# Two chained expert layers on one core: the first layer's input products by Strassen's algorithm, two plain tiles at the change of layers, and buffers laid out anew

## The chip, the core and the metric

The kernel runs on one core of one Trainium2 chip. The core has a TensorE (PE in the rows, with its weight loads as PEld), a VectorE (DVE), a ScalarE (ACT), a GpSimd (POOL) and a SyncE (SP) that issues the DMAs here. The metric is the device time of one execution in microseconds (us); the time of a kernel is the median of its runs.

## The reference

Attention by clusters (a query sees the keys of its own cluster), whose output has 1536 rows (tokens) of 512, and then two dense expert layers:

```
def _moe_ref(x, w_in, w_out):            # layer 1: x 1536x512, w_in 512x2048, w_out 2048x512
    h = x @ w_in
    g = h - np.tanh(h)
    return g @ w_out
...
def _moe2_ref(x, w_gate, w_val, w_out):  # layer 2: w_gate, w_val 512x1536, w_out 1536x512
    gate = 1.0 / (1.0 + np.exp(-(x @ w_gate)))
    val = x @ w_val
    return gate * val @ w_out
```

The weights come as 64-bit floats.

## The kernel before

**Numbers and tiles.** Every matrix product is made of three TensorE matmuls: each factor is split in a high and a low part, and high by high, high by low and low by high are summed in PSUM. A split is two instructions, a copy to the high part on ACT and a subtraction for the low part on POOL or DVE. Activations lie transposed, features on partitions, as `xh` and `xl` (high and low), in four column tiles of 384 tokens (`CH`, c = 0 to 3; c = 0, 1 are pair p = 0 and c = 2, 3 pair p = 1). Hidden features go in tiles of 128, two to a group: eight groups in layer 1 (`NG1`), six in layer 2 (`NG2`). `KD` = 4 is the number of 128-row pieces of the inner dimension of the input products, `KH` = 2 half of it.

**Layer 1** (`moe1_up`, `moe1_down`). For a group g and a column tile c, `up` makes two PSUM tiles of 12 matmuls (L927, in `mm3`), each of 128x384. ACT takes tanh, DVE subtracts (L962), and `pair_of` splits the result on ACT (L950) and POOL (L951). `moe1_down` multiplies by `w_out`: four PSUM tiles of 6 matmuls, which DVE adds to accumulators in SBUF (L1000). A column tile of a group thus takes 24 + 24 = 48 matmuls, and layer 1 takes 8 x 4 x 48 = 1536.

**Layer 2** (`moe2_up`, `moe2_down`). A pair of column tiles and one tile each of gate and value form a product of 2 x 2 blocks, which Strassen's algorithm (in Winograd's form) makes with seven block products in place of eight: 7 x 6 = 42 matmuls (L1136) in place of 48. The right factors are B11, B21, B22 and the sums T1 to T4 of the accumulators, which `inputs` makes and splits (L1041, L1044, L1054); the left factors are A11, A12, A22 and the sums S1 to S4 of the weights, made by `weights2` (L1087, L1089, L1098). The block sums come together in three PSUM banks X, Y and Z: the first product is copied out of X by ACT (L1152) before the third one goes into X, and so on.

**Weights.** `cut_piece` loads a piece of 128x256 doubles and makes 32-bit floats of it with three DVE instructions (L874 to L876); it is then split.

**Order.** The body only lists tasks with an engine, a modelled cost, a priority and dependencies; `Planner.run` sets the order of the instructions on every engine from these, engine by engine, before the program is built. `Z0` and `rank` set the priorities. `b4_left`, `raw_left`, `x_left` and their like say what an SBUF or PSUM buffer becomes when its first use is over, which is why the rows name the layers' operands by the attention's tiles: stk, hlq, hlk, oht, w, sum (split operands), pf, rawv (values before their split), pt, xn (accumulators, outputs), vs, rawq, xtq (weights); over_left, over_right and sm are PSUM banks.

## Time and profile before

| what | value |
|---|---|
| time, median of 3 runs | 812.18 us (811.35 to 816.54) |
| the profiled execution's own time | 816.28 us |
| its span, first to last instruction | 814.4 us |
| TensorE busy in the span | 792.9 us (97%) |
| VectorE, ScalarE, GpSimd busy | 550.2, 412.2, 493.6 us |
| mean granted TensorE clock | 0.985 of full speed |

Attention takes about the first 262 us of the span, layer 1 runs to about 525 us and layer 2 to the end. Matmuls overlap, so a busy TensorE is one that always had a matmul in flight; how many matmuls it ends in a stretch is told by the counts beside the busy times.

### The profile page before, as it was taken

What the parts mean: (1) busy time and instruction counts of PE and PEld (TensorE: products, weight loads), DVE (VectorE), ACT (ScalarE), POOL (GpSimd) and SP (SyncE); (2) the same over time, 40 slices, a digit from 0 to 9 for tenths busy, and PEclk for the clock granted to TensorE, in tenths of its full rate; (3) what the DMA queues carried; (4) which work ended last, traced back from release to release, by engine and by line L of the source; (5) the groups of instructions that cost most, each with busy time, mean ns of one, the idle gap of its engine ahead of it and who ended that gap; (6) DMA issues with size and microseconds to landing.
All of it is one profiled execution on the core that took longest, in us unless ns stands there. A gap on an engine that the chain in (4) does not pass through costs nothing.

```text
span 814.4 us, 15955 instructions
## 1 busy us (share of the span) xinstructions
PE 792.9 (97%) x6027; PEld 742.7 (91%) x6027; DVE 550.2 (68%) x1048; ACT 412.2 (51%) x796; POOL 493.6 (61%) x521
## 2 busy tenths in 40 slices
PE   8999999999899999999999999989999999999998
PEld 7879799888779999999999999979898999999896
DVE  3887987697797946765856643896474586747634
ACT  4177778878678534333233323556552534345240
POOL 4267677977779535442434536799483876649541
PEclk9988999999899999999999999999999999999999
DMA  8876566655353502211202100022230222202004
GB/s 187 205 188 138 128 152 138 141 128 140 88 151 112 173 31 95 104 52 53 78 13 66 52 14 1 1 65 81 85 103 18 66 97 73 77 27 79 27 1 155
DMA packets 66268, 72.94 MB, mean 90 GB/s; under 512 B 30256, under 2 KB 46736, under 8 KB 66192
## 3 DMA queue, kind: packets, MB, share of 16 engines
q1 hardware_dynamic: 66192, 71.93, 31.8%
q8 instruction: 47, 0.77, 0.4%
q14 instruction: 29, 0.24, 0.1%
HBM read 48.27 MB, written 3.15 MB: 63 GB/s over the span
## 4 chain that ended last, share of the span: by engine, by line
PE 84%; DVE 9%; ACT 2%; issue 2%; DMA 2%; POOL 1%; SPq 1%; DVEq 0%; ACTq 0%; POOLq 0%
PE over_left L927 20%; PE over_left L1136 13%; PE over_right L927 12%; PE sm L927 10%; PE over_right L1136 4%; PE sm L1136 3%; DVE finr L625 2%; PE sm L406 2%; PE sm L687 2%; PE sm L688 2%; PE sm L689 2%; PE bc L621 1%; PE sm L515 1%; PE ba L656 1%; PE bb L621 1%
## 5 line engine op out<-in xcount | busy, mean ns | idle before, releaser
L670 POOL TENSOR_TENSOR pt<-pf,pt 128x768 f16<-128x768 f32 x79 | 135.4, 1728 | 57.2 <-ACT pt L660 36.5
L951 POOL TENSOR_TENSOR stk<-pf,stk 128x384 fp32r<-128x384 f32 x35 | 35.6, 1018 | 61.5 <-ACT stk L950 60.4
L687 PE MATMUL sm<-vs,pt 128*128 128x65 f16 x576 | 63.7, 198 | 0.5 <-DVE mt L631 0.5
L687 PEld LDWEIGHTS <-pt 128*128 128x128 f16 x576 | 54.7, 99 | 9.2 <-issue 9.0
L688 PE MATMUL sm<-vs,pt 128*128 128x64 f16 x576 | 63.1, 199 | 0.0
L689 PE MATMUL sm<-vs,pt 128*128 128x65 f16 x576 | 62.7, 195 | 0.0
L688 PEld LDWEIGHTS <-pt 128*128 128x128 f16 x576 | 55.4, 100 | 0.7 <-issue 0.5
L689 PEld LDWEIGHTS <-pt 128*128 128x128 f16 x576 | 55.3, 102 | 0.0
L927 PE MATMUL over_left<-xh,stk 128*128 128x384 f32 x196 | 53.9, 334 | 0.0
L1136 PE MATMUL over_left<-xh,w 128*128 128x384 f32 x166 | 50.0, 338 | 1.7 <-DVE pf L1174 1.7
L1136 PE MATMUL over_left<-sum,w 128*128 128x384 f32 x206 | 44.5, 339 | 0.0
L625 DVE TENSOR_REDUCE finr<-bc 128x1 fp32r<-128x768 f32 x35 | 33.3, 950 | 16.1 <-PE bc L621 14.3
L927 PE MATMUL over_left<-xh,w 128*128 128x384 f32 x140 | 39.4, 337 | 0.3 <-DVE pf L962 0.3
L950 ACT ACTIVATE stk<-pf 128x384 fp32r<-128x384 f32 x39 | 20.4, 524 | 36.4 <-DVE pf L962 20.7
L625 DVE TENSOR_REDUCE finr<-bb 128x1 fp32r<-128x768 f32 x35 | 33.2, 949 | 7.6 <-PE bb L621 7.5
L927 PE MATMUL over_left<-stk,stk 128*128 128x384 f32 (+1 forms) x152 | 36.7, 362 | 0.9 <-ACT stk L950 0.8
L1136 PEld LDWEIGHTS over_left<-sum,w 128*128 128x128 f32 x206 | 36.9, 188 | 0.6 <-ACT rawv L1152 0.2
L962 DVE TENSOR_TENSOR pf<-over_left,pf 128x384 f32<-128x384 f32 x31 | 17.1, 555 | 28.3 <-ACT pf L961 28.2
L927 PE MATMUL sm<-stk,stk 128*128 128x512 f32 (+1 forms) x150 | 36.2, 364 | 0.0
L927 PEld LDWEIGHTS over_left<-xh,stk 128*128 128x128 f32 x196 | 35.8, 188 | 0.0
L660 ACT ACTIVATE pf<-ba 128x768 f32<-128x768 f32 x35 | 28.8, 822 | 13.1 <-PE ba L657 10.8
L660 ACT ACTIVATE pf<-bc 128x768 f32<-128x768 f32 x30 | 24.7, 823 | 16.1 <-PE bc L657 13.6
(515 smaller groups left out, 2750.8 us busy)
## 6 DMA issues: line engine op xcount, KB each, us to landing
vs<-in_moe_w_out_dram SPq DMA_DIRECT2D x25, 256.0 KB, 2.4
stk<-hlq SPq DMA_DIRECT2D x32, 192.0 KB, 2.7
stk<-hlk SPq DMA_DIRECT2D x16, 384.0 KB, 5.6
vs<-in_moe_w_gate_dram SPq DMA_DIRECT2D x18, 256.0 KB, 2.7
vs<-in_moe_w_val_dram SPq DMA_DIRECT2D x18, 256.0 KB
xtk<-in_moe_w_out_dram SPq DMA_DIRECT2D x16, 256.0 KB, 2.4
rawq<-in_q_dram SPq DMA_DIRECT2D x16, 192.0 KB, 4.7
rawk<-in_k_dram SPq DMA_DIRECT2D x16, 192.0 KB, 4.5
```

What stands on the lines that cost most here:

```text
L406: nc.tensor.matmul(tiles["sm", 1][:, 0:P], busy, busy, start=True, stop=True)
L625: rd.append(use(mx, add(DVE, c_dve(S), z + t, lambda t=t, mx=mx: nc.vector.tensor_reduce(at(mh)[:, t:t + 1], at(mx)[:, :, 0:HALF], axis=AX ...
L660: nc.scalar.activation(o.rearrange("p (j n) -> p j n", j=2), at(st)[:, :, 0:HALF], AF.Exp, scale=scale)
L670: lambda nce=nc.vector if on_v else nc.gpsimd, pf=pf, pt=pt: nce.tensor_tensor(at(pt)[:, 1], at(pf), at(pt)[:, 0], op=ALU.subtract), [e0, e1])
L687: nc.tensor.matmul(oview()[:, t], ph, vv[:, 0:D + 1], start=(kt == 0), stop=False)
L688: nc.tensor.matmul(oview()[:, t, 0:D], ph, vv[:, D + 1:2 * D + 1], start=False, stop=False)
L689: nc.tensor.matmul(oview()[:, t], plo, vv[:, 0:D + 1], start=False, stop=(kt == T - 1))
L927: nc.tensor.matmul(ps, a, b, start=(i == 0), stop=(i == n - 1))
L950: a = add(ACT, c_acts(CH), z, lambda: nc.scalar.activation(hi(), src(), AF.Copy), deps, take)
L951: b = add(POOL, c_pool(CH), z, lambda: nc.gpsimd.tensor_tensor(lo(), src(), hi(), op=ALU.subtract), [a])
L962: b = add(DVE, c_dve(CH), z, lambda ps=ps, th=th, g32=g32: nc.vector.tensor_tensor(at(g32), at(ps)[:, 0:CH], at(th), op=ALU.subtract), [a] ...
L1136: nc.tensor.matmul(at(bank[to])[:, 0:CH], lh, rh, start=start and i == 0, stop=stop and i == 3 * KH - 1, skip_group_check=True)
```

## The change

The first two of layer 1's eight groups stay as they were. For the other six, `inputs1` makes T1 to T4 out of the attention's output (POOL adds high and low part back together, DVE subtracts, ACT, DVE and POOL split), `weights2` makes A and S out of `w_in`, and `blocks` (the former `moe2_up`) makes the 2 x 2 blocks of two feature tiles and two column tiles by seven products; its new branch `one` takes h - tanh(h) with `less_tanh` and splits with `give`. At the change of layers the first two feature tiles of layer 2 (`NPL2`) are made plainly by `plain_up`, with 4 x 12 matmuls for a pair, from B11, B21, B12 and B22 alone; `inputs` first splits these four, and makes T1 to T4 in `sums`, listed after the second plain tile. Products of layer 1's down part and of layer 2 now share one set of six PSUM banks (`h2`), and two others serve `cut_piece` (`mid`). The accumulators come from tiles of twice the size (`twins`), the weights' raw buffers of the attention's time go to a pool that is closed and laid out anew (`rx`, `ry`), and `B4_TO` lists what the weight buffers become. Priorities have new constants.

```diff
-    ZLOWP=2.75, SEMS=1.0, TC=0.456, TW=0.74, M2=1, ZQK=0.25, ZMS=-28.375, Z0=47.548, HB=94, NB4=5, ROWS=0.0155,
-    VB=9.164, RAWL=2.2)
+    ZLOWP=2.75, SEMS=1.0, TC=0.456, TW=0.74, M2=1, ZQK=0.25, ZMS=-28.375, Z0=53.342, HB=94, NB4=5, ROWS=0.0155,
+    VB=9.164, RAWL=2.2, NMID=2, NPL2=2, W1L=0.7, D1L=0.322, W2L=1.623, D2L=-0.754, ZI=7.032, ZJ=1.1)
...
+            twin = left_p.tile([P, 2, 2, S], F16, name=f"ptt_{i}")
+            twins.append(twin)
+            for j in range(2):
+                new("pt", twin[:, j])
...
+    B4_TO = ["wb"] * 4 + ["wo"] * 2 + ["wb", "t", "t", "t", "wb"]
...
         x_gone.append(i)
-        return [new("h2" if len(x_gone) <= 2 else "x2", tiles["x", i])]
+        return [new("mid" if len(x_gone) <= NMID else "h2", tiles["x", i])]
...
         t = use_w(w, add(PE, C_UP, step(C_UP), mm_, w[1] + deps, [ps]))
+        ups_done.setdefault(c, []).append(t)
...
+    def inputs1(p):
+        c0, c1 = 2 * p, 2 * p + 1
+        where = {"B11": (0, c0), "B21": (KH, c0), "B22": (KH, c1), "T1": (0, c1), "B12": (0, c1)}
+        there = xt_done[2] + xt_done[3]
...
+        def of_tile(k):
+            val, ready = {}, {}
+            z = z0 + PRM["ZI"] + 0.1 * k
+            for n, kind in (("B11", "th"), ("B12", "g32"), ("B22", "th"), ("B21", "g32")):
+                val[n] = Slot(kind)
+                ready[n] = use(val[n], add(POOL, c_pool(CH), z, lambda n=n, v=val[n]: nc.gpsimd.tensor_tensor(
+                    at(v), place(n)(0, k).bitcast(F32), place(n)(1, k).bitcast(F32), op=ALU.add),
+                    there + sums_done, [val[n]]))
...
+            sum_("T1", "B12", "B11", "B11")
+            sum_("T3", "B22", "B12", "B12", [ready["T1"]])
+            sum_("T2", "B22", "T1", "B22", [ready["T3"]])
+            sum_("T4", "B21", "T2", "B21")
+            sums_done[:] = [ready["T4"]]
+            split("T2", DVE)
+            split("T4", POOL)
+            split("T3", DVE)
+
+            split("T1", DVE, ups_done[c1])
+
+        for k in range(KH):
+            of_tile(k)
+        return pairs
...
-        s11 = split("B11", POOL)
-        s21 = split("B21", POOL)
-        s22 = split("B22", POOL)
-        sum_("T1", "B12", "B11", "B11", s11)
-        sum_("T3", "B22", "B12", "B12", ready["T1"])
-        sum_("T2", "B22", "T1", "B22", s22 + ready["T3"])
-        sum_("T4", "B21", "T2", "B21", s21)
-        split("T2", DVE)
-
-        split("T1", DVE)
-        split("T3", POOL)
-        split("T4", POOL)
-        return pairs
+        done = [split(n, on) for n, on in (("B11", POOL), ("B21", DVE), ("B12", POOL), ("B22", DVE))]
+
+        def sums(used):
+
+            sum_("T1", "B12", "B11", "B11", done[0] + done[2])
+            sum_("T3", "B22", "B12", "B12", ready["T1"] + done[3])
+            sum_("T2", "B22", "T1", "B22", ready["T3"])
+            sum_("T4", "B21", "T2", "B21", done[1])
+            split("T2", DVE)
+            split("T1", POOL, used)
+            split("T3", DVE)
+            split("T4", POOL)
+
+        return pairs, sums
...
-        for i, (n, w, k) in enumerate((("A11", w_gate, 0), ("A12", w_gate, 1), ("A21", w_val, 0), ("A22", w_val, 1))):
+        for i, (n, w, f, k) in enumerate((("A11", w0, f0, 0), ("A12", w0, f0, 1), ("A21", w1, f1, 0), ("A22", w1, f1, 1))):
...
+        if plain:
+            split("A21")
+            split("A22")
+            cut_done[:] = pairs["A22"][1]
+            return pairs
...
+    def plain_up(A, B, p, gs, fi):
+
+        users = []
+        for c, names in ((2 * p, ("B11", "B21")), (2 * p + 1, ("B12", "B22"))):
...
+                t = add(PE, C_UP, step(C_UP), mm_, [d for (_, w), (_, b, _) in terms for d in w + b], [bank])
...
+            gate, t0 = half(1)
+            x = Slot("tmp")
+            th = add(ACT, c_act(CH), rank[0], lambda gate=gate, x=x: nc.scalar.activation(
+                at(x), at(gate)[:, 0:CH], AF.Sigmoid), [t0], [x])
+            use(gate, th)
+            value, t1 = half(2)
+            m = add(DVE, c_dve(CH), rank[0], lambda value=value, x=x: nc.vector.tensor_tensor(
+                at(x), at(value)[:, 0:CH], at(x), op=ALU.mult), [th, t1])
+            use(value, m)
+            use(x, th, m)
...
+        return users
...
+        def less_tanh(src, dst, dep, on, take=()):
+            th = Slot("tmp")
+            a = add(ACT, c_act(CH), rank[0], lambda: nc.scalar.activation(at(th), src(), AF.Tanh), [dep], [th])
+            b = add(on, c_pool(CH) if on == POOL else c_dve(CH), rank[0], lambda: (
+                nc.gpsimd if on == POOL else nc.vector).tensor_tensor(at(dst), src(), at(th), op=ALU.subtract), [a], take)
+            use(th, b)
+            return use(dst, b)
...
-        th0 = sigmoid(a, add_to(a, "Z", [ta, m2]))
+        t11 = add_to(a, "Z", [ta, m2])
+        if one:
+            give(c0, 0, a, less_tanh(lambda: at(a), a, t11, POOL))
+        else:
+            th0 = sigmoid(a, t11)
...
-        v1 = add_to(u, "Y", [tu, m5])
+        t22 = add_to(u, "Y", [tu, m5])
+        if one:
+            give(c1, 1, u, less_tanh(lambda: at(u), u, t22, POOL))
         m4 = product("A22", "T4", "X", [tu], True)
-        m3 = product("S4", "B22", "Y", [v1], True)
+        m3 = product("S4", "B22", "Y", [t22], True)
+        if one:
+            x = Slot("tmp")
+            t21 = less_tanh(lambda: ps("X"), x, m4, DVE, [x])
+            use(bank["X"], t21)
+            give(c0, 1, x, t21)
+            give(c1, 0, b, less_tanh(lambda: at(b), b, add_to(b, "Y", [tb, m3]), POOL))
+            return
...
-    per1 = NCH * (GF * C_UP + KD * C_DN) / 1.9
-    w1 = [(weights(cols(w_in, g), Z0 + (g - 1.3) * per1, "raw", "x" if g else "sm"),
-           weights(rows(w_out, g), Z0 + (g - 1.1) * per1, "raw", "x" if g else "sm")) for g in range(NG1)]
-    Z1 = Z0 + NG1 * per1
+    NPL, NPL2 = 2, PRM["NPL2"]
+    per0 = NCH * (GF * C_UP + KD * C_DN) / 1.9
+    w1 = [(weights(cols(w_in, g), Z0 + (g - 1.3) * per0, "rawx", "x" if g else "sm"),
+           weights(rows(w_out, g), Z0 + (g - 1.1) * per0, "rawx", "x" if g else "sm")) for g in range(NPL)]
+    Z1 = Z0 + NPL * per0
...
-    order1 = [(g, c) for cc in (0, 2) for g in range(2) for c in (cc, cc + 1)] + [(g, c) for g in range(2, NG1) for c in range(NCH)]
-    for g, c in order1:
-        gt = moe1_up(w1[g][0], c, xt_done[c])
-        flush()
-        pend = (w1[g][1], gt, c, g, False)
-    ups = [weights2(f, Z1 + (f - 1.3) * per2, "x" if f < 2 else "x2") for f in range(GF * NG2)]
-    downs = [weights(rows(w_out2, g), Z1 + (GF * g + 0.3) * per2, "raw2", "x2", "wo") for g in range(NG2)]
+        for x in todo:
...
+    for c0 in (0, 2):
+        for g in range(NPL):
+            for c in (c0, c0 + 1):
+                gt = moe1_up(w1[g][0], c, xt_done[c])
+                flush()
+                todo.append((moe1_down, w1[g][1], gt, c, g))
+        x1[c0 // 2] = inputs1(c0 // 2)
+    up1 = [weights2(w_in, GF * g, w_in, GF * g + 1, Z1 + (g - NPL - PRM["W1L"]) * per1, "x" if g == NPL else "mid")
+           for g in range(NPL, NG1)]
+    down1 = [weights(rows(w_out, g), Z1 + (g - NPL - PRM["D1L"]) * per1, "raw2", "mid", "wo") for g in range(NPL, NG1)]
+    ups = [weights2(w_gate, f, w_val, f, Z2 + (f - PRM["W2L"]) * per2, plain=f < NPL2) for f in range(GF * NG2)]
+    downs = [weights(rows(w_out2, g), Z2 + (GF * g - PRM["D2L"]) * per2, "raw2", "mid", "wo") for g in range(NG2)]
+    for g in range(NPL, NG1):
...
+        for p in range(NCH // 2):
+            gs = {c: ((Slot("g"), Slot("g")), []) for c in (2 * p, 2 * p + 1)}
+            blocks(up1[g - NPL], x1[p], p, gs)
+            flush()
+            for c in gs:
+                todo.append((moe1_down, down1[g - NPL], gs[c], c, g, "h2"))
+            if g == NG1 - 1:
+                todo.append((lambda p: x2.update({p: inputs(p)}), p))
     flush()
-    todo = []
     for g in range(NG2):
...
-                moe2_up(ups[GF * g + fi], x2[p], p, gs, fi)
-                for x in todo:
-                    moe2_down(*x)
-                todo = [(downs[g], gs[c], c, g) for c in (2 * p, 2 * p + 1)] if fi == GF - 1 else []
-    for x in todo:
-        moe2_down(*x)
+                f = GF * g + fi
+                if f < NPL2:
+                    used = plain_up(ups[f], x2[p][0], p, gs, fi)
+                    if f == NPL2 - 1:
+                        todo.append((x2[p][1], used))
+                else:
+                    blocks(ups[f], x2[p][0], p, gs, fi)
+                flush()
+                if fi == GF - 1:
+                    todo.extend((moe2_down, downs[g], gs[c], c, g) for c in (2 * p, 2 * p + 1))
+    flush()
```

How the built program's order moves, at three places. The first is TensorE at the start of layer 1's third group. Before, the first output tile's last matmuls and then the second's, of twelve each, from the x parts alone:

```order
L927 MATMUL over_left_3982<-xh,stk_88 128x384 x2
L927 MATMUL over_left_3982<-xl,stk_88 128x384
L927 MATMUL over_left_3982<-xh,stk_88 128x384
L927 MATMUL over_left_3983<-xh,stk_88 128x384
L927 MATMUL over_left_3983<-xl,stk_88 128x384
L927 MATMUL over_left_3983<-xh,stk_88 128x384 x2
```

Now, the end of the first product (bank over_left_3982), the second, of six matmuls, and the third (S2 by T2), which comes back to the first one's bank:

```order
L1288 MATMUL over_left_3982<-xh,stk_87 128x384
L1288 MATMUL over_right_3858<-xh,stk_87 128x384
L1288 MATMUL over_right_3858<-xl,stk_87 128x384
L1288 MATMUL over_right_3858<-xh,stk_87 128x384 x2
L1288 MATMUL over_right_3858<-xl,stk_87 128x384
L1288 MATMUL over_right_3858<-xh,stk_87 128x384
L1288 MATMUL over_left_3982<-sum_4324,stk_87 128x384
L1288 MATMUL over_left_3982<-sum_4325,stk_87 128x384
```

The bank's copy to SBUF has one product's time. The second place is TensorE at the change of layers. Before, the end of layer 2's second product, layer 1's last four down tiles, and the third product, which needs T2 (sum_6365 and its like) of the new activations:

```order
L1136 MATMUL over_left_3985<-xl,stk_88 128x384
L1136 MATMUL over_left_3985<-xh,stk_88 128x384
L927 MATMUL over_left_3984<-stk_86,stk_88 128x384 x6
L927 MATMUL over_right_3860<-stk_86,stk_88 128x384 x6
L927 MATMUL sm_71<-stk_86,stk_88 128x384 x6
L927 MATMUL over_right_3860<-stk_86,stk_88 128x384 x6
L1136 MATMUL over_left_3983<-sum_6365,w_132 128x384
L1136 MATMUL over_left_3983<-sum_6367,w_132 128x384
```

Now layer 1's last down tile is followed by the first plain tile, of B11 and B21 (in xh and xl) alone:

```order
L969 MATMUL over_left_3982<-hlk_125,w_132 128x384
L969 MATMUL over_left_3982<-hlq_122,w_132 128x384
L969 MATMUL over_left_3982<-hlk_125,w_133 128x384
L969 MATMUL sm_71<-xh,ry_4248 128x384
L969 MATMUL sm_71<-xl,ry_4248 128x384
L969 MATMUL sm_71<-xh,w_131 128x384
```

No product with a sum of the new activations stands between layer 1's down tiles any more. The third place is VectorE there, whose L1000 (now L1045) adds to the accumulators. Before, sums (L1054) and splits (L1044) stand among layer 1's own instructions, ahead of the last additions:

```order
L1054 TENSOR_TENSOR pt_108<-pt_104,pt_108 128x768
L1044 TENSOR_TENSOR xl<-xn_114,xh 128x384
L962 TENSOR_TENSOR rawv_92<-over_right_3859,rawv_92 128x384
L1054 TENSOR_TENSOR pt_104<-pt_104,xn_114 128x768
L1054 TENSOR_TENSOR pt_107<-pt_107,pt_104 128x768
L1044 TENSOR_TENSOR sum_6367<-pt_104,sum_6365 128x384
L1044 TENSOR_TENSOR sum_6369<-pt_104,sum_6366 128x384
L962 TENSOR_TENSOR rawv_92<-over_left_3982,rawv_92 128x384
```

Now the additions come with splits of B alone (L1153), and weights' cuts (L916 to L918):

```order
L1045 TENSOR_TENSOR ptt_104<-over_left_3981,ptt_104 128x384
L1153 TENSOR_TENSOR xl<-ptt_105,xh 128x384
L1045 TENSOR_TENSOR ptt_104<-sm_72,ptt_104 128x384
L916 TENSOR_SCALAR over_right_3859<-vs_89 128x256
L917 SCALAR_TENSOR_TENSOR over_right_3859<-vs_89,over_right_3859 128x256
L918 SCALAR_TENSOR_TENSOR vs_89<-vs_89,over_right_3859 128x256
L1153 TENSOR_TENSOR xl<-ptt_104,xh 128x384 x2
L1045 TENSOR_TENSOR ptt_105<-over_right_3858,ptt_105 128x384
```

The sums of 128x768 have moved behind all of layer 1's additions.

## Rows read from the trace of the kernel before

**Rows 1.** The page: the span, and TensorE's busy time, share and instructions.

```profile
span 814.4 us, 15955 instructions
...
PE 792.9 (97%) x6027; PEld 742.7 (91%) x6027; DVE 550.2 (68%) x1048; ACT 412.2 (51%) x796; POOL 493.6 (61%) x521
```

**Rows 2.** Stretches: from:to, length, then each engine's busy us (instructions), clock.

```profile
280.00:500.00 220.00, 220.00 (x1268) 220.00 (x1267) 134.16 (x294) 75.08 (x173) 96.47 (x114) 1.00 0.17 56
...
524.00:548.00 24.00, 20.38 (x97) 17.41 (x96) 22.58 (x40) 14.81 (x32) 22.75 (x21) 0.93 0.14 44
...
570.00:800.00 230.00, 230.00 (x1195) 213.44 (x1194) 137.41 (x285) 100.04 (x228) 142.86 (x177) 1.00 0.19 60
```

**Rows 3.** TensorE's waits, 520 to 550 us: in total, times, longest.

```profile
PE over_left L1136 <- DVE pf L1174: 1.7, 1, 1.7
PE over_left L927 <- ACT stk L950: 0.8, 1, 0.8
PE over_left L1136 <- DVE xl L1044: 0.5, 2, 0.3
PE over_left L1136 <- DVE stk L1044: 0.4, 1, 0.4
PE over_left L927 <- POOL stk L951: 0.2, 1, 0.2
```

**Rows 4.** TensorE's timeline at the change of layers: start, us, line, count, idle before.

```profile
525.49 0.94 PE L927 MATMUL over_left<-stk,stk 128*128 128x384 f32 x4 [0.78 <-ACT stk L950]
...
542.01 0.44 PE L1136 MATMUL over_left<-xh,w 128*128 128x384 f32 x1 [1.71 <-DVE pf L1174]
...
544.45 0.84 PE L1136 MATMUL over_left<-hlq,w 128*128 128x384 f32 x2
```

**Rows 5.** The chain that ended last, 505 to 570 us: start, us, what.

```profile
521.82 2.58 DVE sum L1044 x2
...
540.23 1.26 DVE xn L1054
```

**Rows 6.** Groups by line and form, 262 to 815 us: busy us, mean ns.

```profile
L951 POOL TENSOR_TENSOR stk<-pf,stk 128x384 fp32r<-128x384 f32 x35 | 35.6, 1018 | 61.5 <-ACT stk L950 60.4 <-PE over_left L927 0.8 <-PE over_right L927 0.3
...
L950 ACT ACTIVATE stk<-pf 128x384 fp32r<-128x384 f32 x39 | 20.4, 524 | 36.4 <-DVE pf L962 20.7 <-DVE pf L1174 11.8 <-POOL pf L1177 3.7
...
L1152 ACT ACTIVATE pf<-over_left 128x384 f32<-128x384 f32 x41 | 19.9, 486 | 22.6 <-PE over_left L1136 22.6
...
L1089 POOL TENSOR_TENSOR w<-vs,w 128x256 fp32r<-128x256 f32 x26 | 19.2, 740 | 4.2 <-PE over_left L1136 1.4 <-PE sm L1136 1.4 <-ACT stk L899 0.8
...
L962 DVE TENSOR_TENSOR pf<-over_left,pf 128x384 f32<-128x384 f32 x31 | 17.1, 555 | 28.3 <-ACT pf L961 28.2
...
L1087 ACT ACTIVATE w<-vs 128x256 fp32r<-128x256 f32 x33 | 13.4, 412 | 9.2 <-DVE vs L876 2.7 <-POOL vs L1098 2.3 <-PE over_left L1136 2.3
...
L875 DVE SCALAR_TENSOR_TENSOR over_left<-vs,over_left 128x256 uint32<-128x256 uint32 x30 | 12.9, 429 | 1.0
```

**Rows 7.** POOL's timeline: the attention's last subtraction, and two splits.

```profile
257.07 2.36 POOL L670 TENSOR_TENSOR pt<-pf,pt 128x768 f16<-128x768 f32 x1 [0.93 <-DVE xn L704]
...
522.65 2.62 POOL L1044 TENSOR_TENSOR sum<-pt,sum 128x384 fp32r<-128x384 f32 x2
```

**Rows 8.** DVE's timeline at the same time as the two splits.

```profile
521.75 2.66 DVE L1044 TENSOR_TENSOR sum<-pt,sum 128x384 fp32r<-128x384 f32 x2
```

**Rows 9.** Stretches of the attention with a low clock (last columns: clock, DMA).

```profile
60.00:80.00 20.00, 20.00 (x266) 18.00 (x267) 15.52 (x26) 13.74 (x21) 14.32 (x11) 0.85 0.64 142
...
200.00:220.00 20.00, 17.73 (x236) 15.24 (x236) 16.36 (x25) 13.39 (x20) 16.20 (x11) 0.83 0.29 73
```

**Rows 10.** The first stretch after the attention.

```profile
262.00:280.00 18.00, 17.68 (x123) 17.41 (x120) 16.97 (x43) 11.09 (x26) 13.88 (x18) 1.00 0.52 172
```

More of the change, by code (lines that the diff above doesn't have):

```diff
@@ L883, in f32_of, with weights @@
         return at(cut).bitcast(F32)
-    def weights(src, prio, raw_kind="raw", mid_kind="x", kind="b4"):
+    def weights(src, prio, raw_kind="rawx", mid_kind="x", kind="b4"):
         w = Slot(kind), Slot(kind)
@@ L935, in step @@
         return rank[0]
+    ups_done = {}
     def up(w, f, c, deps):
@@ L1019, in inputs @@
             ("B11", c0, 0), ("B21", c0, 1), ("B12", c1, 0), ("B22", c1, 1))}
-        where = {"B11": (0, c0), "B21": (KH, c0), "B22": (KH, c1), "T1": (0, c1)}
+        where = {"B11": (0, c0), "B21": (KH, c0), "B12": (0, c1), "B22": (KH, c1), "T1": (0, c1)}
         pairs = {}
```

168 lines of the change are left out of this document (121 added, 47 removed).

## The prediction

> **What bounds the kernel now.** The page comes first: TensorE is busy 792.9 of a span of 814.4 us, no other engine over 68% [rows 1]. An average over three stages proves little, so the stretches come next [rows 2]. From 280 to 500 us, in layer 1, TensorE is busy 220.00 of 220 us and ends 1268 matmuls: 0.1735 us for one of 128x384. VectorE has 134, GpSimd 96 and ScalarE 75 us there. From 570 to 800 us, in layer 2, where the blocks are already Strassen's, TensorE again has 230.00 of 230 us; GpSimd has 143 (62%), VectorE 137 (60%), ScalarE 100 (43%). So in both layers time follows the number of matmuls. (Its 1195 matmuls don't give that length, as layer 2's down part has matmuls of 128x512; no sum below uses them.)
>
> Between the two, from 524 to 548 us, only 97 matmuls end in 24 us [rows 2]. They are worth 97 x 0.1735 = 16.8 us, so the change of layers loses **7.2 us**. The view of TensorE's waits names 1.7 + 0.8 + 0.5 + 0.4 + 0.2 = 3.6 us of it [rows 3]; the timeline shows the 0.78 and 1.71 in place, and behind them two matmuls that take 0.84 us instead of 0.35 [rows 4], at a mean granted clock of 0.93 against 1.00 before and after [rows 2], between the levels of 1.2 and 2.4 GHz. 0.07 x 24 = 1.7 us is that clock's part; the other 1.9 are short waits. The chain of waits there runs over VectorE's splits (2.58) and sums (1.26) of the new activations [rows 5]: the third product, which needs T2, has nothing left in front of it.
>
> Attention ends with the same instructions in the same order; what differs there is where buffers lie. Its stretches at clock 0.85 and 0.83 [rows 9] make this execution one of the long ones: 816.28 us, 1.9 over its span, where the median is 812.18. I keep attention's time, and take the difference off the median.
>
> **The change part by part.**
>
> *Matmuls.* In six groups of layer 1, for two pairs, the up part takes 7 x 6 = 42 in place of 8 x 6 = 48: 6 x 2 x 6 = 72 fewer. The two plain tiles of layer 2 give back 2 x 2 x 6 = 24. Net 48 x 0.1735 = **-8.3 us**. TensorE being full where they go [rows 2], all of that counts, if the other engines keep up.
>
> *Steady groups of layer 1.* A group (two pairs) now has 2 x 42 + 96 = 180 matmuls, 31.2 us. GpSimd: 8 low parts and 6 subtractions of tanh, 14 x 1.018, and 15 instructions on weights of 256 columns, 15 x 0.740 [rows 6]: 25.4 us, 81% (it was 8 + 8 of these, 14.1 us of 33.3). VectorE: 24 x 0.555 and 24 x 0.429 for the cuts [rows 6]: 23.6 us, 76%. ScalarE: 22 of about 0.51 and 11 of 0.412 [rows 6]: 15.7 us, 50%. None is full, but GpSimd is at 81% where layer 2 shows 62% without loss, so the trace has no row for this load. Its cost is between 0 (as 570 to 800) and what its queue would make late; I take 0 for a group, since nothing waits for GpSimd's last results for at least a down tile.
>
> *X's copies.* A first product must leave bank X within the one product, 6 x 0.1735 = 1.04 us, that stands between. The copy takes 0.486 [rows 6]; behind one other 0.524 of ScalarE it is 1.01. That is tight, but layer 2 has the same three copies in each block, and from 570 to 800 it pays nothing. Zero, with the bad end as a rival.
>
> *Seam from plain to Strassen in layer 1.* `inputs1` adds 8 sums of two parts and splits for each pair on GpSimd. It comes free of attention at 257.07 + 2.36 = 259.4 us [rows 7], and has 36 x 1.018 + 22 x 0.740 = 53 us [rows 6] until the second pair's last split: 312 us. TensorE comes to it after the first two groups, 384 matmuls behind 262.6: 329 us. So 17 us of plain work cover it; the sums issue no DMA, and the row pieces of `w_in` are loaded as 128x2x256 pieces instead, as many issues on SP as before. But here VectorE adds from two operands in SBUF, 28 times, beside GpSimd. The only rows with such a pair show GpSimd's two splits at 2.62 us, 1.31 each instead of 1.018, while VectorE's two take 2.66 [rows 7, 8], 1.33 each instead of 0.555 with one operand in PSUM [rows 6]. 28 x 0.29 = 8.1 us more for GpSimd: inside the 17.
>
> The Trainium skill bears on this: "SBUF — State Buffer", section "SBUF: two separate sides", says that VectorE with two SBUF inputs and GpSimd hold a shared port pair in turn, the other one blocked for the whole instruction. The stretch of 1.018 to 1.31 agrees in direction; it is less than the two in turn (1.018 + 0.555 = 1.57). By the rule the sum for the seam would be 28 x 0.555 = 15.5 us of GpSimd, still within the 17, by little.
>
> *Start of layer 1.* Before, the first stretch after attention kept TensorE busy 17.68 of 18 us [rows 10]. The same plain groups start there: 0.3 us stays.
>
> *Change of layers.* Now four down tiles of layer 1 for each column tile lie behind seven products, and then a plain tile that needs only B11 and B21 split. Some twelve PSUM tiles of six matmuls, 12 x 1.04 = 12.5 us, stand on TensorE between the first pair's last down tile and that plain tile, and two splits of both kinds take 2.6 us even stretched [rows 7]. The sums and T splits, 5 us or more on VectorE by the chain [rows 5], lie behind 16 plain PSUM tiles of 12 matmuls, 16 x 2.08 = 33 us; T1's split, which waits for a plain tile's last reader, has about 20 us. What queues behind that wait on GpSimd is T4's split and weights' low parts for a later tile. So the old loss goes: **-7.2 us**. VectorE gets the four rounds of additions in a row with splits; what is late next is the first split itself.
>
> *New stalls.* The trace shows no seam of this kind. Between 0 (as in both steady stretches) and 7.2 (as the old seam) I take one wait as the 0.78 ahead of the down tiles [rows 4] with the 0.2 of GpSimd's split [rows 3], 1.0, and the 0.3 of a stretch at a start [rows 10]: **+1.3 us**, nearer to 0 because both seams have more plain work in front than the sums need.
>
> Sum: -8.3 - 7.2 + 1.3 = **-14.2 us**. This execution, 816.28, would be 802.1; the median, 812.18, becomes **798.0 us**.
>
> **Rivals.**
>
> A, *the loss at the change of layers only moves.* The plain tiles themselves come too early for the last additions, or the half clock is paid anyway behind some wait. For it: additions, splits and cuts all go over VectorE, which had 22.58 of 24 us there, and GpSimd 22.75 [rows 2]. Against it: 33 us of work that needs no sum. With all 7.2 kept, the saving is 8.3 less 0.3: 804.2 us; I put the case at 804.
>
> B, *GpSimd becomes the bound of layer 1's six groups.* If every instruction of its 25.4 us were stretched as the two splits were, by 1.31/1.018, it would need 32.7 us for a group against TensorE's 31.2: 1.5 x 6 = 9 us, 798 + 9 = 807. Against it: in the steady blocks no VectorE instruction reads two operands from SBUF (subtractions and additions read a bank, the cuts too), so the rows' cause [rows 7, 8] is there at the seams alone. The Trainium skill's rule (the same section) has that same condition, so by it this rival stays out.
>
> C, *slower than before: ScalarE late for bank X.* In layer 1 tanh and split copies of four results come to ScalarE in each block, beside the weights' copies. If each of the three copies of the 12 blocks, 36, stood behind one instruction of 0.52 us more than TensorE leaves it, that is 36 x 0.52 = 18.7 us; less the 15.5 of the two gains it makes 812.2 + 3.2 = 815.4. It decides from 15.5 / 36 = 0.43 us a wait, and half clock behind so many waits would add to it. Against it: layer 2's blocks, with sigmoids in the same place, wait nowhere long enough to move 230.00 of 230 [rows 2].
>
> That fewer matmuls bring nothing would need another bound than TensorE in layer 1; 220.00 of 220 us with VectorE at 61% [rows 2] leaves that no room.
>
> **How the numbers follow.** Forecast 798, 78%; A 10%, 804; B 6%, 807; C 6%, 815. The range: down to the old loss gone, no new stall, 812.2 - 15.5 = 796.7, and the runs' own spread below their median (0.8) and a little of attention's clock [rows 9], 794.5; up over A with the same spread, 806. About 1% is what a measurement of this kernel tells from no change, as its runs spread over 5 us: faster is below 804.1, slower above 820.3. The forecast and half of A, 83%, are faster; the rest of A, B and 2 of C's 6%, 13%, are the same; 4% are slower, C with waits above (820.3 - 796.7) / 36 = 0.66 us, which half clock would bring about.
>
> **What the profile after would show.** 48 fewer matmuls, TensorE full from 280 us to the change of layers and on, GpSimd near 80% and VectorE near 75% in the six groups; layer 1 ends some 12 us earlier (72 x 0.1735 = 12.5). At the change no wait for VectorE over 1 us, and clock 1.00. A shows as waits of a plain tile for a split of VectorE or GpSimd; B as TensorE waiting for GpSimd's low parts in every group; C as waits on bank X for the copy on ScalarE. The forecast is wrong if the first Strassen block of layer 1 waits for `inputs1` or for weights, if stalls of half a microsecond come in every block, or if the new places of buffers change attention.

## The result, and the profile after

The changed kernel takes **801.25 us** (median of 4 runs, 800.67 to 804.67) where the kernel before takes 812.94 (4 runs): a ratio of 0.9859, 95% interval 0.9815 to 0.9902. A second set of 6 runs of it, beside runs of before, gave 0.9868 (0.9841 to 0.9896), 804.07 against 814.19. It is faster by 1.4%, 11.7 us (10.1 in the second set); 798.0 with 14.2 less was forecast, in a range of 794.5 to 806.

The page of the changed kernel, its span and busy times (compare [rows 1]): 48 matmuls fewer, and more work on every other engine.

```profile
span 799.3 us, 15929 instructions
...
PE 779.2 (97%) x5979; PEld 731.4 (92%) x5979; DVE 573.3 (72%) x1076; ACT 439.4 (55%) x852; POOL 567.3 (71%) x597
```

Stretches of the changed kernel, in the columns of [rows 2]: the start of layer 1, its seam from plain groups to Strassen groups, the Strassen groups, the change of layers, and layer 2.

```profile
260.00:280.00 20.00, 19.28 (x113) 18.96 (x112) 16.90 (x32) 12.18 (x28) 17.92 (x20) 1.00 0.16 57
300.00:320.00 20.00, 18.24 (x103) 17.60 (x103) 13.45 (x18) 10.51 (x25) 13.80 (x13) 1.00 0.00 1
340.00:540.00 200.00, 200.00 (x1149) 200.00 (x1148) 153.14 (x328) 100.94 (x224) 163.29 (x188) 1.00 0.23 73
540.00:560.00 20.00, 19.64 (x101) 17.82 (x100) 17.24 (x33) 13.39 (x33) 19.92 (x20) 1.00 0.29 91
600.00:760.00 160.00, 160.00 (x831) 148.83 (x830) 104.39 (x216) 66.09 (x151) 98.68 (x123) 1.00 0.19 62
```

TensorE is full for the whole of 340 to 540 us, with GpSimd at 163 of 200 us (82%) and VectorE at 77%. The change of layers has lost its hole: 19.64 of 20 us at clock 1.00, where before it was 20.38 of 24 at 0.93. The holes are now at 260 and 300 us. TensorE's waits of the changed kernel after 255 us, in the form of [rows 3]:

```profile
PE over_right L969 <- DVE pf L1007: 1.7, 1, 1.7
PE over_left L969 <- ACT pf L1006: 0.7, 1, 0.7
PE over_right L1288 <- ACT pf L1304: 0.4, 1, 0.4
```

To account for all of it, take the part behind the attention: from the end of its last score matmul (254.41 us before, 250.68 after) to the end of the span. It is 559.97 us before and 548.58 after, 11.4 less. Going from each matmul's start to the next one's, every excess over 0.1736 us (384 columns; 0.2288 for 512) is a gap where it is above 0.03 us, and a slow matmul where it is less. A gap in this sense is a wait, or a matmul stretched by a lower clock behind one.

| us | before | after | difference |
|---|---|---|---|
| 2544 and 2496 matmuls of 384 columns x 0.1736 (431 of 512 the same) | 441.64 | 433.31 | -8.33 |
| gaps at the start of layer 1 (240 to 280 us) | 0.43 | 1.34 | +0.91 |
| gaps at layer 1's seam (300 to 340 us) | 0 | 2.61 | +2.61 |
| gaps at the change of layers | 7.41 | 0.97 | -6.44 |
| smaller gaps elsewhere | 0.72 | 0.01 | -0.71 |
| matmuls slower by under 0.03 us each, in sum | 2.11 | 3.24 | +1.13 |
| transposes and the rest | 5.01 | 4.45 | -0.56 |
| in all | | | -11.4 |

The attention was 3.7 us shorter in this profiled execution; that is its clock and not the change (last section).

### The profile page after: what moved, and what is told of

It reads as the page before. It is cut to its first block, busy times and chain, and to the rows that moved or that the text cites. A ratio compares the mean times of both kernels' runs of the same rounds, so it can differ in the third digit from the quotient of the medians.

```text
span 799.3 us, 15929 instructions
## 1 busy us (share of the span) xinstructions
PE 779.2 (97%) x5979; PEld 731.4 (92%) x5979; DVE 573.3 (72%) x1076; ACT 439.4 (55%) x852; POOL 567.3 (71%) x597
## 4 chain that ended last, share of the span: by engine, by line
PE 77%; DVE 10%; POOL 3%; issue 3%; DMA 3%; ACT 2%; SPq 1%; DVEq 0%; POOLq 0%; ACTq 0%
PE over_left L969 16%; PE over_left L1288 14%; PE sm L1288 11%; PE sm L969 9%; PE over_right L969 5%; PE over_right L1288 4%; DVE finr L637 2%; PE sm L418 2%; PE sm L699 2%; PE sm L700 2%; PE sm L701 2%; PE bb L633 1%; DVE vs L614 1%; PE ba L668 1%; PE bc L633 1%
## 5 line engine op out<-in xcount | busy, mean ns | idle before, releaser
L682 POOL TENSOR_TENSOR pt<-pf,pt 128x768 f16<-128x768 f32 x45 | 77.5, 1736 | 34.3 <-ACT pt L672 18.5
L682 POOL TENSOR_TENSOR ptt<-pf,ptt 128x768 f16<-128x768 f32 x34 | 58.2, 1717 | 19.7 <-ACT ptt L672 15.6
L996 POOL TENSOR_TENSOR stk<-pf,hlq 128x384 fp32r<-128x384 f32 x25 | 26.1, 1045 | 33.2 <-ACT hlq L995 33.2
L699 PE MATMUL sm<-vs,pt 128*128 128x65 f16 x330 | 43.7, 196 | 0.4 <-DVE mt L643 0.4
L701 PE MATMUL sm<-vs,pt 128*128 128x65 f16 x330 | 43.0, 193 | 0.0
L969 PE MATMUL over_left<-stk,w 128*128 128x384 f32 x158 | 40.1, 335 | 0.0
L699 PEld LDWEIGHTS <-pt 128*128 128x128 f16 x330 | 31.2, 97 | 6.2 <-issue 6.0
L672 ACT ACTIVATE pf<-ba 128x768 f32<-128x768 f32 x35 | 28.8, 823 | 13.3 <-PE ba L669 11.4
L1308 DVE TENSOR_TENSOR pf<-over_left,pf 128x384 f32<-128x384 f32 x32 | 17.7, 553 | 25.2 <-ACT pf L1304 11.4
L969 PE MATMUL over_left<-w,stk 128*128 128x512 f32 x118 | 34.9, 392 | 0.0
L700 PE MATMUL sm<-vs,ptt 128*128 128x64 f16 x246 | 34.8, 197 | 0.0
L699 PE MATMUL sm<-vs,ptt 128*128 128x65 f16 x246 | 34.7, 195 | 0.0
L701 PE MATMUL sm<-vs,ptt 128*128 128x65 f16 x246 | 34.4, 194 | 0.0
L672 ACT ACTIVATE pf<-bc 128x768 f32<-128x768 f32 x30 | 24.8, 826 | 14.9 <-PE bc L669 12.4
L996 POOL TENSOR_TENSOR oht<-pf,stk 128x384 fp32r<-128x384 f32 x25 | 25.6, 1025 | 9.9 <-ACT stk L995 9.2
L700 PEld LDWEIGHTS <-pt 128*128 128x128 f16 x330 | 31.5, 98 | 0.6 <-issue 0.5
L701 PEld LDWEIGHTS <-pt 128*128 128x128 f16 x330 | 31.7, 100 | 0.0
```

What stands on the lines that cost most here:

```text
L672: nc.scalar.activation(o.rearrange("p (j n) -> p j n", j=2), at(st)[:, :, 0:HALF], AF.Exp, scale=scale)
L682: lambda nce=nc.vector if on_v else nc.gpsimd, pf=pf, pt=pt: nce.tensor_tensor(at(pt)[:, 1], at(pf), at(pt)[:, 0], op=ALU.subtract), [e0, e1])
L699: nc.tensor.matmul(oview()[:, t], ph, vv[:, 0:D + 1], start=(kt == 0), stop=False)
L700: nc.tensor.matmul(oview()[:, t, 0:D], ph, vv[:, D + 1:2 * D + 1], start=False, stop=False)
L701: nc.tensor.matmul(oview()[:, t], plo, vv[:, 0:D + 1], start=False, stop=(kt == T - 1))
L969: nc.tensor.matmul(ps, a, b, start=(i == 0), stop=(i == n - 1))
```

## The experiments

All are edits of the changed kernel. "Stage" is the part behind the attention as above, which doesn't move with the attention's clock; gaps are those of TensorE by place. Stage and gaps are of one profiled execution each. The ratio is to the kernel before's runs beside each version, whose median was 813.2 to 814.2 us for all rows but the first two; ratios and stages compare better than medians.

| run | median us (range) | ratio to before, 95% | stage | gaps: all | seam | change |
|---|---|---|---|---|---|---|
| before | 812.94 (811.35 to 816.54) | | 559.97 | 8.56 | 0 | 7.41 |
| the change | 801.25 (800.67 to 804.67) | 0.9859 (0.9815 to 0.9902) | 548.58 | 4.93 | 2.61 | 0.97 |
| changed_again | 804.07 (800.35 to 804.88) | 0.9868 (0.9841 to 0.9896) | 548.65 | 5.00 | 2.75 | 0.89 |
| all_plain1 | 814.83 (814.09 to 819.67) | 1.0033 (1.0012 to 1.0054) | 562.20 | 6.49 | 0 | 5.04 |
| no_plain2 | 812.80 (808.77 to 814.09) | 0.9974 (0.9952 to 0.9995) | 556.90 | 17.29 | 2.62 | 13.33 |
| one_plain2 | 806.50 (805.87 to 810.08) | 0.9920 (0.9884 to 0.9957) | 554.38 | 12.55 | 2.63 | 8.56 |
| one_plain_group | 822.89 (821.27 to 824.18) | 1.0114 (1.0080 to 1.0149) | 569.06 | 27.25 | 24.81 | 1.25 |
| more_gpsimd | 827.69 (821.45 to 828.10) | 1.0157 (1.0109 to 1.0204) | 571.69 | 27.72 | 2.35 | 8.11 |
| copies_twice | 808.47 (806.71 to 811.67) | 0.9939 (0.9916 to 0.9961) | 555.45 | 11.48 | 2.79 | 2.15 |
| tanh_on_vector | 805.64 (804.71 to 807.24) | 0.9903 (0.9870 to 0.9935) | 552.81 | 8.99 | 2.61 | 2.77 |
| sums_on_vector | 801.50 (799.76 to 804.21) | 0.9854 (0.9822 to 0.9885) | 547.33 | 3.63 | 1.19 | 1.09 |
| sums_half | 801.83 (800.76 to 809.05) | 0.9866 (0.9833 to 0.9900) | 548.54 | 4.79 | 2.37 | 1.05 |
| sums_later | 805.42 (803.64 to 808.37) | 0.9896 (0.9863 to 0.9929) | 550.41 | 6.79 | 3.98 | 1.29 |
| measured_costs | 803.24 (802.29 to 805.16) | 0.9867 (0.9839 to 0.9895) | 549.54 | 5.80 | 2.27 | 1.20 |

**Each half alone.** First all of layer 1 plain (`plain1` is `moe1_up` with the weights' buffers of `weights2`):

```diff
+    NQ = 8
...
-        x1[c0 // 2] = inputs1(c0 // 2)
...
-    for g in range(NPL, NG1):
+    for g in range(NPL, NQ):
+        for p in range(NCH // 2):
+            for c in (2 * p, 2 * p + 1):
+                gt = plain1(up1[g - NPL], c)
...
+    for g in range(NQ, NG1):
```

> The changed kernel with all eight groups of layer 1 plain: only the two plain tiles of layer 2 and the new buffers are left of the change. Theory (time follows the matmuls, the plain tiles take the loss at the change of layers from 7.2 to about 1 us, and the seam inside layer 1 costs 2.6 us): against before 24 more matmuls, +4.2, and -6.2 at the change: 810.9; against the changed kernel 72 more matmuls, +12.5, less the seam's 2.6: 811.2. Rival (the loss at the change only moves into the plain tiles): 812.9 + 4.2 = 817. TensorE's gaps between the layers should sum to about 1 us by the theory, to 7 by the rival.

It came out at 814.83, no faster than before. The 72 matmuls are there: 562.20 - 548.58 = 13.6 is 12.5 for them, less the seam's 2.6, less 0.4 of slower matmuls, and 4.1 more at the change, whose gaps are 5.04 and not 1. They sit in layer 2's first down tiles, where TensorE waits for GpSimd's low parts:

```profile
PE over_right L969 <- POOL stk L996: 1.5, 1, 1.5
PE over_right L969 <- POOL w L943: 0.7, 1, 0.7
```

Neither theory's number held (1 and 7 us). The plain tiles alone save 2.4 us of gaps here and cost 4.2 in matmuls.

Then the change without plain tiles (B12 is not split then, and the sums are listed right behind layer 1's last additions):

```diff
-    ... NPL2=2, ...
+    ... NPL2=0, ...
...
-                todo.append((lambda p: x2.update({p: inputs(p)}), p))
+                todo.append((lambda p: (x2.update({p: inputs(p)}), x2[p][1]([])), p))
```

> The changed kernel without plain tiles at the change of layers: the sums of the new activations are listed right behind layer 1's last additions, and B12 is not split. Theory: 24 matmuls fewer, -4.2, and the loss at the change comes back to about 7 from 1: +6.2, so 801.3 + 2.0 = 803.3, with waits for VectorE's sums and splits as before. Rival (the down tiles behind seven products suffice, the plain tiles are not needed): 797, with no wait over 1 us there.

It takes 812.80 us, where the theory had 803.3: the loss that came back is 13.33 us, nearly twice the kernel before's. The rival (not needed) is out. A part of the loss is the lower clock behind the waits, 0.74 on average from 520 to 540 us. That stretch, then VectorE of no_plain2 at the longest wait, then TensorE:

```profile
520.00:540.00 20.00, 13.85 (x52) 11.94 (x51) 19.76 (x26) 13.09 (x28) 14.95 (x13) 0.74 0.11 39
```
```profile
522.94 1.27 DVE L1163 TENSOR_TENSOR ptt<-ptt,ptt 128x768 f32<-128x768 f32 x1
524.13 0.54 DVE L1308 TENSOR_TENSOR pf<-sm,pf 128x384 f32<-128x384 f32 x1
```
```profile
524.73 0.69 PE L1288 MATMUL sm<-xh,ry 128*128 128x384 f32 x1 [4.55 <-DVE pf L1308]
```

The addition that frees bank `sm` for layer 1's last blocks stands behind sums (L1163) of the next layer and weights' cuts in VectorE's queue, and TensorE stood 4.55 us. With one plain tile (`NPL2=1`):

> The changed kernel with one plain tile at the change of layers instead of two. Theory (the plain tiles are cover for the chain of sums and splits, which without them kept TensorE waiting some 13 us; one tile of both pairs is 8 x 2.08 = 16.7 us, which is more): 12 matmuls fewer, -2.1, loss at the change about 1 us as with two: 799.2. Rival (the chain needs more than one tile's time, VectorE and GpSimd being full there): half the 13 us comes back, 801.3 - 2.1 + 6 = 805, with waits for VectorE's splits ahead of the third product.

The rival came out: 806.5, 8.56 us of gaps at the change. TensorE's waits of one_plain2 there, and ScalarE:

```profile
PE over_left L1288 <- ACT pf L1304: 4.1, 1, 4.1
...
PE over_left L1288 <- ACT rawv L1304: 1.2, 1, 1.2
```
```profile
533.48 0.94 ACT L1150 ACTIVATE sum<-ptt 128x384 fp32r<-128x384 f32 x2 [4.28 <-DVE ptt L1163]
...
537.49 0.47 ACT L1304 ACTIVATE pf<-over_left 128x384 f32<-128x384 f32 x1
```

ScalarE stands 4.28 us in a split of a sum that VectorE has not made; the copy out of bank X (L1304) is behind it in the queue. So a tile's 16.7 us is no cover by itself: what counts is when the sums come through VectorE. Fewer plain tiles mean less cover and also an earlier place of the sums in the queues; these runs don't tell the two apart.

**How much plain work layer 1 needs in front** (`NPL = 1`):

> The changed kernel with one plain group in layer 1 instead of two, seven by Strassen. 12 matmuls fewer, -2.1. Theory (the seam in layer 1 is bounded by GpSimd and VectorE working off inputs1; GpSimd's 53 us of work had 17 us of slack under two groups, 67 us): under one group, 33 us, some 15 us of it are not covered: waits of 8 to 15 us, 807 to 814. Rival (the seam's 2.3 us are an accident of the order on VectorE and the work itself is small): 799.2.

Theory, and more than it: 24.8 us at the seam. TensorE's longest wait is again for the copy out of bank X:

```profile
PE over_right L1288 <- ACT pf L1304: 8.4, 3, 5.4
```

Not all of it is `inputs1`. ScalarE has splits of sums and the weights' copies ahead of that copy, and stands up to 2.34 us for weights that VectorE is still cutting; VectorE, with cuts and sums in turn, is busy 18.87 of 20 us from 300 to 320, and the granted clock is 0.75 there.

**GpSimd's margin in the steady groups.** In `less_tanh`, once in a block:

```diff
+            if on == POOL and len(extra) < 1:
+                extra.append(1)
+                for _ in range(2):
+                    a = add(POOL, c_pool(CH), rank[0], lambda: nc.gpsimd.tensor_tensor(
+                        at(th), src(), at(th), op=ALU.subtract), [a])
```

> The changed kernel with two more subtractions of 128x384 on GpSimd in each of layer 1's Strassen blocks (tanh is turned into the result and back before it is used), 4 x 1.018 = 4.1 us for a group: GpSimd's load goes from 81% to 29.5 of 31.2 us, 94%. Theory (its queue has real slack, the steady groups lose nothing): 801.3 to 802.5. Rival (GpSimd is as good as the bound, what looks idle is waiting in its chain): most of 24 x 1.018 = 24 us shows, 810 to 825, as waits of TensorE for GpSimd's low parts in every group.

The rival, and a little more than its range: 24.4 us more work on GpSimd made the stage 23.1 us longer. 15.9 of the gaps lie in the Strassen groups, 8.1 at the change (0.97 without it). The stretch of the groups in more_gpsimd, and two of its groups of TensorE rows with what ended their idle time:

```profile
340.00:540.00 200.00, 190.49 (x1057) 182.83 (x1056) 140.72 (x291) 88.31 (x202) 167.60 (x193) 1.00 0.21 64
```
```profile
L1288 PE MATMUL over_left<-xh,stk 128*128 128x384 f32 x42 | 13.4, 346 | 1.4 <-POOL stk L1199 1.4
L1288 PE MATMUL over_left<-sum,stk 128*128 128x384 f32 x40 | 9.1, 349 | 0.9 <-POOL stk L1199 0.9
```

GpSimd is 84% busy and TensorE already waits for its low parts of weights (L1199). What looks idle is time in which it waits in its own chain, as in the changed kernel's groups from 360 to 520 us:

```profile
L1318 POOL TENSOR_TENSOR pf<-pf,pf 128x384 f32<-128x384 f32 x10 | 10.1, 1014 | 4.3 <-ACT pf L1316 4.3
L1318 POOL TENSOR_TENSOR rawv<-rawv,pf 128x384 f32<-128x384 f32 x9 | 9.2, 1021 | 5.7 <-ACT pf L1316 5.7
L1318 POOL TENSOR_TENSOR pf<-pf,rawv 128x384 f32<-128x384 f32 x7 | 7.1, 1012 | 8.2 <-ACT rawv L1316 8.2
```

These waits for ScalarE's tanh are 18.2 of the 31 us that GpSimd is idle there, before 13 of 28 such subtractions. The added work stands in this chain, between tanh and the low part; whether as much of it elsewhere in GpSimd's queue would cost the same, no run shows. The reverse edit moves the three subtractions to VectorE (`less_tanh(..., DVE)` at the three places with POOL):

> The changed kernel with the three subtractions of tanh in each of layer 1's Strassen blocks on VectorE instead of GpSimd: GpSimd's load falls by 6.1 us for a group (to some 62%), VectorE's rises by 6 x 0.55 to 6 x 1.2 us, since they read two operands in SBUF beside GpSimd. Theory (GpSimd is near its limit in these groups but costs nothing yet, and VectorE at 27 to 31 of 31.2 us would be at its own): 802 to 806, with waits for VectorE. Rival (GpSimd's load is what costs in layer 1 and at the change): 799 to 800.

805.64, as the theory had it: GpSimd falls to 132 of 200 us, VectorE rises to 174 (87%), and TensorE waits for VectorE at the first group (1.0 and 0.4 us) and at the change (1.3 and 0.5).

```profile
340.00:540.00 200.00, 198.62 (x1135) 197.53 (x1134) 173.61 (x363) 101.25 (x225) 132.12 (x155) 1.00 0.24 74
```

**Bank X's copies** (`copy_out` in layer 1's blocks adds the same activation once more):

> The changed kernel with each copy out of bank X made twice by ScalarE in layer 1's Strassen blocks, 36 more instructions of 0.49 us: one product, 1.04 us, has to cover 2 x 0.49 and the way there and back. Theory (the single copy has some 0.4 us of slack, and each doubled one is late by 0.1 to 0.3 us, and half clock may follow): 36 x 0.1 to 0.3 = 4 to 11 us, 805 to 812. Rival (other instructions of ScalarE or the down tiles between products cover it): 801 to 802.

808.47, inside the theory's range, for another reason: not 36 late copies, but 5.1 us in one place (340 to 380), where a weight's copy stands in ScalarE's longer queue and the granted clock is 0.91 behind the wait (360 to 380), and 1.2 more at the change.

```profile
PE over_right L1288 <- ACT w L1197: 1.6, 1, 1.6
```

From 380 to 540 us TensorE is full with doubled copies. They are covered.

```profile
380.00:540.00 160.00, 160.00 (x918) 160.00 (x917) 123.30 (x260) 89.67 (x204) 132.74 (x153) 1.00 0.23 71
```

**The seam in layer 1.** In the changed kernel the chain of waits there is:

```profile
308.25 1.36 POOL rawv L1084
...
309.64 1.38 DVE pf L1090
...
311.11 1.17 DVE rawv L1090
312.28 0.48 DVE pf L1007
...
312.81 2.37 PE over_right L969 x12
```

GpSimd adds high and low part (L1084), VectorE makes two sums of them (L1090), and only then subtracts tanh for a plain tile (L1007), which frees TensorE's bank. Four edits tried to take that apart: the additions on VectorE (`add(DVE, ...)`, `nc.vector` at L1084), for both pairs and for the second alone; sums later (`ZI=9.0`); and the planned costs set to the measured durations.

> The changed kernel with the 16 additions of high and low part in inputs1 on VectorE instead of GpSimd. Theory (TensorE's 1.7 us wait at 312 us comes because VectorE's queue stands before a sum that waits for GpSimd's additions, which VectorE's own instructions with two SBUF inputs stretch): the wait goes, -1 to -2 us, 799.3 to 800.3. Rival (VectorE has too much to do at that seam): 16 x 0.55 = 8.8 us more on it, the wait grows to 3 us or more, 803 or above.

> The changed kernel with the additions of high and low part on VectorE for the second pair alone (8 of 16). Theory (the plain tile's subtraction stood behind the second pair's sums, which waited for GpSimd's additions): the 1.7 us wait goes as with all 16 moved, -1 to -2 us, 799.3 to 800.3. Rival (it took VectorE's sums of both pairs being free of GpSimd): the wait stays, 801.3.

> The changed kernel with the constant that sets the priority of inputs1's sums and splits (ZI) at 9 instead of 7.032, so that they come later among the plain groups. Theory (the plain tile's subtraction stands behind sums in VectorE's queue): fewer sums ahead of it, the wait gets shorter by 0 to 1.9 us, 799.4 to 801.3, if the first blocks do not wait for their sums in turn. Rival (the wait is one for a free bank whatever the order): 801.3, the same 1.7 us.

> The changed kernel with the costs of inputs1's instructions, from which the order is planned, set to what the trace shows beside each other: additions on GpSimd 1.3 us (planned 0.96), sums on VectorE 1.2 (planned 0.47), splits 1.2 and 0.8. Nothing is computed otherwise; the order on the engines is another. Theory (TensorE's waits at the seam in layer 1 come because the order was made for sums of half their length, so that a plain tile's subtraction stands behind them): the seam's 2.6 us fall below 1.3, 799.5 to 800.5. Rival (the seam has that much work whatever the order, and a better one for the plain tile makes the first Strassen blocks wait): 801 to 806.

Moving all 16 took 1.4 us off the seam (stage 547.33 against 548.58), as expected; its median can't be told from the change's. The other three went against the theory. sums_half lost the 1.7 us wait and got waits of 0.9 and 0.4 for GpSimd's low parts instead, 2.37 in all. sums_later made the first Strassen blocks wait 3.2 us for copies out of X, behind splits and weights' copies on ScalarE. measured_costs has no such wait for the subtraction, and 2.27 us of gaps among the first Strassen blocks instead (342 to 350 us), besides 1.0 us more at the start of layer 1. The waits of sums_half, sums_later and measured_costs:

```profile
PE sm L969 <- POOL hlq L996: 0.9, 1, 0.9
...
PE over_right L969 <- POOL oht L996: 0.4, 1, 0.4
```
```profile
PE over_left L1288 <- ACT pf L1304: 3.2, 3, 1.6
```
```profile
PE over_left L1288 <- DVE xnt L1045: 0.9, 1, 0.9
```

So the subtraction's place in the queue isn't the cause of the seam's loss, only its form. Four orders with additions on GpSimd (the change's, sums_half with eight of the 16, sums_later, measured_costs) pay 2.3 to 4.0 us; the one that leaves them all to VectorE pays 1.2. VectorE's sums in the changed kernel, and in sums_on_vector, two forms of each (durations in ns, least, median, greatest):

```profile
L1090 DVE TENSOR_TENSOR pf<-pf,pf x4: 541/908/1375, 273.8 to 303.3; 128x384 f32<-128x384 f32 x4
L1090 DVE TENSOR_TENSOR pf<-pf x4: 909/1294/2354, 276.3 to 304.0; 128x384 f32<-128x384 f32 x4
```
```profile
L1090 DVE TENSOR_TENSOR pf<-pf,pf x5: 543/557/981, 286.3 to 309.7; 128x384 f32<-128x384 f32 x5
L1090 DVE TENSOR_TENSOR pf<-pf x4: 546/556/1089, 279.7 to 308.2; 128x384 f32<-128x384 f32 x4
```

The same sum takes 0.56 us in the median with the additions gone from GpSimd, and 0.91 and 1.29 beside them. All 16 sums together take 16.7 us in the changed kernel and 10.6 in sums_on_vector. That the two engines' blocking of each other (last section) makes up the 1.4 us agrees with this, but no run here separates it from GpSimd's mere relief. changed_again has the same three waits in the same places as the first profile:

> The changed kernel itself, for a comparison on one chip with the two others. 801.3, TensorE's gaps after the attention 4.9 us in all, if the waits of 0.7 and 1.7 us in layer 1 are part of the order of the program; a rival, that they are an accident of one execution, gives other waits in other places.

No version tried beats the change by more than can be measured; sums_on_vector has the shortest stage.

## Why the prediction was right, point by point

**Matmuls, -8.3: right.** Layers 1 and 2 are full before and after, and the count's worth appears (-8.3; with all_plain1's 12.5 its stage comes out too).

**Change of layers, -7.2: right in size, half right in its reason.** 7.41 us of gaps became 0.97. That sums and splits need plain work in front is shown by 13.33, 8.56 and 0.97 us with no, one and two plain tiles. But the down tiles behind seven products were counted as cover too, and with them alone no_plain2 loses 13.33 us; and all_plain1 shows 5.04 us with both plain tiles where layer 1 is plain. Why the Strassen groups leave the change smoother stays open: the waits there name GpSimd, and all_plain1 also cuts layer 1's weights in other banks than the change does. One row was misread there: two matmuls in 0.84 us [rows 4] stand against 0.51 for such a pair at clock 1.00, not 0.35; no sum rests on it.

**New stalls, +1.3: the term that was mis-sized.** They came to 5.6: 0.9 more at the start of layer 1, 2.6 at its seam, 0.97 at the change, 1.1 in slower matmuls. The 1.3 less of small things elsewhere was not foreseen, and makes the sum -11.4 instead of -10.1, where -14.2 was forecast; that part of the closeness is luck. Two steps failed in this term. *"The same plain groups start there: 0.3 us stays"*: VectorE of the changed kernel now splits the attention's last transposes (L736) ahead of the subtraction that frees a bank,

```profile
262.99 1.02 DVE L736 TENSOR_TENSOR xl<-sm,xh 128x384 fp32r<-128x384 f32 x2
263.93 0.55 DVE L1007 TENSOR_TENSOR pf<-over_left,pf 128x384 f32<-128x384 f32 x1
```

and TensorE waits 0.7 us. (Its row names ScalarE's L1006, which ends within 0.01 us of the subtraction; in sums_on_vector the row of this wait names L1007.) The attention's own instructions stand in the order of before on each engine, as the prediction has it, but layer 1's are put among them otherwise. all_plain1 has the same wait, so it isn't the Strassen work (read, not tested by itself). *"17 us of plain work cover it"*: the seam was costed as GpSimd's work laid end to end, done at 312 us, with TensorE there at 329; 308 and 325 with the attention 3.7 us shorter. In the changed kernel GpSimd's last split of a T ends at 320.7,

```profile
319.72 1.02 POOL L1100 TENSOR_TENSOR stk<-pf,w 128x384 fp32r<-128x384 f32 x1 [0.60 <-ACT w L1097]
```

and TensorE's first Strassen product begins at 321.3: of the 17 us some 0.5 were left. GpSimd's work was not the error: blocking by VectorE cost it 5.1 us from 271 to 341 (above 1.02 and 0.74 us an instruction), where 8.1 was reckoned. It stood waiting, busy 13.80 of 20 us from 300 to 320, mostly for ScalarE's high parts of the plain groups' results, and these for VectorE's subtraction of tanh behind its sums:

```profile
312.78 0.53 ACT L995 ACTIVATE stk<-pf 128x384 fp32r<-128x384 f32 x1 [4.27 <-DVE pf L1007]
```

VectorE's own part was put at nothing: its 28 instructions on two operands in SBUF took 12.5 us more than 0.55 each, in the queue that also holds the plain tiles' subtractions. The first Strassen block itself shows no named wait for `inputs1`, the sign of being wrong that the prediction gave; a plain tile ahead of it does. one_plain_group, 24.8 us where 15 was expected, fits with less cover than 17, but doesn't size it, as its weights were late too.

The two engines in turn were reckoned as 1.018 + 0.555 = 1.57 us, so that the rows' 1.31 and 1.33 [rows 7, 8] looked like less. They are the turns themselves (last section).

**Rival B**, GpSimd as the bound: it didn't happen, 200.00 of 200 us at 82%. The reason given held: in the groups, from 380 to 500 us, no instruction of VectorE reads two operands in SBUF, and GpSimd's subtractions take their usual 1.01 to 1.02 us. But the bound was set too high. B was to cost something from 31.2 us a group on; more_gpsimd, at 25.4 + 4.1 = 29.5, paid nearly all of what was added, two thirds of it in the groups. "Busy 81%" was read as 19% of room, and there was hardly any in this chain.

**Rival C**, copies out of X: out in the blocks, as doubled copies cost nothing there; its mechanism, a copy behind another instruction in ScalarE's queue, is what one_plain2, one_plain_group and sums_later pay, once, at a seam.

**Rival A**: out; the loss went from the change, and 2.6 of it appeared in another place.

## What to carry to other kernels

Where a faster algorithm needs sums of its inputs first, count plain work that needs none of them as part of its price, and try the amount: here one tile too few cost 5 us (one_plain2), one group too few 22 us. An engine at 82% in an order full of chains can be at its limit; add a known amount of work to the chain and see what of that shows. Price a seam on every queue it goes through, not on the busiest engine alone. At a seam, look for what frees TensorE's banks, and what stands ahead of it in each in-order queue: moving the order about mostly moves the wait.
